# The recurrent part of a chunked mLSTM kernel turned around: v stationary, weights streaming, state term in PSUM, exponent bias on ScalarE

## The chip, the cores and the metric

The kernel runs on one core of one Trainium2 chip. The metric is the device time of one execution in microseconds (us). For each kernel one execution was also recorded by the hardware profiler; what is read from a trace is from that one execution, and what is said of times is from all runs.

## The reference

Two blocks follow one another. The first is a recurrent cell over 768 steps for 4 batches of 8 heads of 40 features:

```python
for t in range(S):                                   # S = 768, per batch and head, D = 40
    m_new  = maximum(f[t] + m, i[t])
    f_stab, i_stab = exp(f[t] + m - m_new), exp(i[t] - m_new);  m = m_new
    C = f_stab * C + i_stab * outer(v[t], k[t])      # 40 x 40 state
    n = f_stab * n + i_stab * k[t]
    y[t] = sigmoid(o[t]) * (C @ q[t]) / maximum(abs(n @ q[t]), 1.0)
# ... then, with x = y as (4, 768, 320):
u  = x + real(fft(fft(x, axis=1), axis=2))
un = (u - mean(u)) / sqrt(var(u) + 1e-6)
out = u + maximum(un @ w_ch1, 0) @ w_ch2             # 320 -> 1280 -> 320
```

## The kernel before

The cell is computed in 6 chunks of 128 steps per batch: inside a chunk as a masked product of scores and weights, between chunks through the state C. All heads of a batch go through one chunk together. The order of the program is batch 0 of the cell, the conversion of the feed-forward weights from float64, batch 1 of the cell, and then Fourier part and feed-forward part batch by batch, with the cell of batches 2 and 3 between them. A scheduler moves instructions, so that parts of neighbouring batches overlap.

This is the chunk, the part that the change touches (`hip` is 0 or 1 for the head of a pair: even heads lie in partitions 0 to 39, odd ones in 64 to 103):

```python
Mb = mbp.tile([L, H, L], FP, name="Mb", tag="Mb")          # running maximum, the same in every partition
nc.sync.dma_start(out=Mb, in_=M_d[c, heads, :].unsqueeze(0).to_broadcast([L, H, L]))
W = wp.tile([L, H, L], FP, name="W", tag="W")
nc.vector.tensor_tensor(out=W, in0=colT[:, c, 0, heads].unsqueeze(2).to_broadcast([L, H, L]), in1=Mb,
                        op=OP.subtract)
nc.gpsimd.affine_select(out=W, in_=W, compare_op=OP.is_ge, fill=MASKED, base=0, pattern=[[0, H], [1, L]],
                        channel_multiplier=-1)
nc.scalar.activation(out=W, in_=W, func=AF.Exp)
for hip in range(2):
    r = slice(hip * 64, hip * 64 + D)
    ps = ps_s.tile([L, NP, L], FP, name="ps", tag="ps")
    for p in range(NP):                                    # scores k x q
        nc.tensor.matmul(ps[:, p, :], qk[r, 1, p, :], qk[r, 0, p, :], start=True, stop=True)
    Wv = W.rearrange("p (pr two) t -> p pr two t", two=2)[:, :, hip, :]
    nc.vector.tensor_tensor(out=Wv, in0=ps, in1=Wv, op=OP.mult)
h1 = tp.tile([L, H, D1], FP, name="h1", tag="h1")
if c > 0:                                                  # the state's share
    pn = ps_h.tile([L, NP, 2 * D1], FP, name="pn", tag="ph")
    for p in range(NP):
        nc.tensor.matmul(pn[:, p, :], qk[:, 0, p, :], C[:, p].rearrange("p a b -> p (a b)"),
                         start=True, stop=True)
    # ... h1 = pn x g on VectorE
ph = ps_h.tile([L, H, D1], FP, name="ph", tag="ph")
for h in range(H):                                         # W loaded, v (41 columns) streams
    nc.tensor.matmul(ph[:, h, :], W[:, h, :], v1[:, h, :], start=True, stop=True)
# ... h1 = h1 + ph on VectorE
# ... vw = v x weight on GpSimd; pc = k x vw; C = C x decay + pc, both on VectorE
# ... den = 1 / max(|h1[:, :, 40]|, 1) on VectorE; so = so x den on GpSimd; x = h1 x so on VectorE
```

## Time and profile before

| | kernel before |
|---|---|
| median of 4 runs | 728.56 us (723.77 to 735.60) |
| profiled run, span | 733.6 us |
| TensorE, VectorE, ScalarE, GpSimd busy | 647.7, 288.7, 110.6, 125.5 us |
| half clock after the first clock record (162.1 us) | 95.7 us |

The traces record two values of TensorE's granted clock, 1.00 (full clock) and 0.50 (half clock). The runs of the kernel before differ by over 2%, and this follows the clock of TensorE. Among seven runs made beside e1 to e4, the fastest, 719.03 us, came with a mean granted clock of 0.959, and the slowest of those that count as fast, 727.73 us, with 0.945. A mean lower by 0.014 over some 723 us is about 20 us more at half clock, and the time grew by 8.7 us. So a microsecond at half clock costs this kernel about 0.43 us, an estimate.

The stages in the tables below are cut by events that both kernels have: "batch 0" ends with the last write of its x, "conversion" with the last conversion instruction on VectorE, "batch 1" with the first product pu of batch 0's Fourier part. "Batch 2 head" is from there to the first feed-forward product pm, "FF 0" the two feed-forward blocks, "batch 2 tail" from the end of their po to the next pu. Batch 3 and FF 1 are cut in the same way, and "rest" is all after it.

### The profile page before, as it was taken

To read this page: it belongs to the slowest core of one execution; us is meant where nothing else is said; L and a number is where in the kernel's file an instruction comes from. 1 tells how busy PE (TensorE), PEld (TensorE's weight loads), DVE (VectorE), ACT (ScalarE), POOL (GpSimd) and SP (SyncE) were. 2 spreads that over 40 slices of the span, in tenths; PEclk is the share of its full clock that TensorE was granted. 3 is DMA by queue.
4 is the path that set the end of the run, shared out by engine and by line. 5 is a ranking of instruction groups with operands and counts; after the bars stand their busy time and mean duration, and the time that the engine had idled before them with its cause. 6 is when DMAs were issued, how large, how long until landed. Compare 5 with 4: busy or idle time off the path is not lost.

```text
span 733.6 us, 6949 instructions
## 1 busy us (share of the span) xinstructions
PE 647.7 (88%) x2732; PEld 431.5 (59%) x2732; DVE 288.7 (39%) x570; ACT 110.6 (15%) x193; POOL 125.5 (17%) x109
## 2 busy tenths in 40 slices
PE   4978321389999999999999999999989999989998
PEld 3867311368677464687684464787645546645545
DVE  6454599997656101145543111154421011330110
ACT  4011143214131101001202101002010100011010
POOL 3121276662232000021302000020200000000000
PEclk9999999999895999986975999957999999999999
DMA  7354145625332000032211000010000000000000
GB/s 229 122 172 172 45 127 173 202 82 185 115 125 86 27 19 27 10 101 86 82 46 48 0 27 1 22 42 1 1 0 10 18 0 28 1 0 0 28 0 28
DMA packets 16113, 45.60 MB, mean 62 GB/s; under 512 B 1968, under 2 KB 5264, under 8 KB 15952
## 3 DMA queue, kind: packets, MB, share of 16 engines
q1 hardware_dynamic: 16080, 45.15, 19.0%
q8 instruction: 22, 0.36, 0.2%
q14 instruction: 11, 0.09, 0.0%
HBM read 41.11 MB, written 4.03 MB: 62 GB/s over the span
## 4 chain that ended last, share of the span: by engine, by line
PE 84%; DVE 10%; issue 4%; ACT 1%; DMA 0%; POOL 0%; DVEq 0%; ACTq 0%; POOLq 0%
PE pm L350 26%; PE po L362 18%; PE pu L322 9%; PE ph L219 8%; PE ps L205 8%; PE pz L300 6%; PE pn L213 4%; DVE m L164 2%; PE pzt L308 2%; PE put L342 2%; PE pc L232 2%; DVE m L168 1%; DVE e L163 1%; DVE e L169 1%; DVE e L160 1%
## 5 line engine op out<-in xcount | busy, mean ns | idle before, releaser
L350 PE MATMUL pm<-unT,w_sb 128*128 128x384 f32 (+1 forms) x480 | 194.2, 536 | 0.6 <-ACT unT L343 0.6
L350 PEld LDWEIGHTS pm<-unT,w_sb 128*128 128x128 f32 (+1 forms) x480 | 80.7, 194 | 111.1 <-issue 87.2
L362 PE MATMUL po<-w_sb,hT 128*128 128x320 f32 x480 | 131.3, 434 | 0.0
L219 PE MATMUL ph<-kvt,W 128*128 128x41 f32 x384 | 71.5, 352 | 50.0 <-DVE W L207 40.9
L362 PEld LDWEIGHTS po<-w_sb,hT 128*128 128x128 f32 x480 | 90.5, 190 | 41.1 <-issue 4.4
L219 PEld LDWEIGHTS ph<-kvt,W 128*128 128x128 f32 x384 | 68.1, 265 | 57.5 <-DVE W L207 43.0
L205 PE MATMUL ps<-qk 40*128 40x128 f32 x384 | 76.4, 383 | 15.1 <-DMA qk<-in_qkT 15.1
L354 DVE TENSOR_SCALAR hT<-pm 128x384 f32<-128x384 f32 x40 | 22.3, 558 | 165.1 <-PE pm L350 165.1
L205 PEld LDWEIGHTS ps<-qk 40*128 40x128 f32 x384 | 62.7, 267 | 20.6 <-issue 16.4
L365 DVE TENSOR_TENSOR ot<-po,u 128x320 f32<-128x320 f32 x24 | 11.8, 492 | 118.4 <-PE po L362 118.4
L322 PE MATMUL pu<-dd_sb,Z 128*128 128x320 f32 x192 | 56.3, 435 | 0.0
L227 POOL TENSOR_TENSOR vw<-kvt,colT 128x328 f32<-128x328 f32 x20 | 15.9, 794 | 207.3 <-issue 195.5
L199 ACT ACTIVATE W<-W 128x1024 f32<-128x1024 f32 x24 | 25.2, 1058 | 155.7 <-POOL W L197 155.7
L300 PE MATMUL pz<-ds_sb,eo 128*128 128x386 f32 (+1 forms) x96 | 45.8, 619 | 1.4 <-ACT Zt L277 1.0
L322 PEld LDWEIGHTS pu<-dd_sb,Z 128*128 128x128 f32 x192 | 36.1, 190 | 15.4 <-issue 0.8
L356 ACT ACTIVATE hT<-pm 128x384 f32<-128x384 f32 x40 | 19.6, 491 | 156.3 <-PE pm L350 156.3
L197 POOL TENSOR_SCALAR_AFFINE_SELECT W<-W 128x1024 f32<-128x1024 f32 x24 | 27.9, 1164 | 77.5 <-DVE W L195 30.7
L213 PEld LDWEIGHTS pn<-C,qk 128*128 128x128 f32 x160 | 31.8, 288 | 8.3 <-issue 7.6
L213 PE MATMUL pn<-C,qk 128*128 128x82 f32 x160 | 33.4, 378 | 2.1 <-DVE C L237 2.1
L207 DVE TENSOR_TENSOR W<-ps,W 128x512 f32<-128x512 f32 x48 | 32.0, 682 | 6.7 <-PE ps L205 3.7
L249 POOL TENSOR_TENSOR so<-so,den 128x320 f32<-128x320 f32 x24 | 20.0, 833 | 79.1 <-DVE den L247 79.1
L195 DVE TENSOR_TENSOR W<-colT,Mb 128x1024 f32<-128x1024 f32 x24 | 31.0, 1291 | 0.0
(84 smaller groups left out, 471.6 us busy)
## 6 DMA issues: line engine op xcount, KB each, us to landing
Mb<-M_d SPq DMA_DIRECT2D x24, 512.0 KB
kvt<-in_kv SPq DMA_DIRECT2D x24, 324.0 KB
qk<-in_qkT SPq DMA_DIRECT2D x48, 160.0 KB
raw<-in_w SPq DMA_DIRECT2D x9, 640.0 KB
so<-in_o SPq DMA_DIRECT2D x4, 960.0 KB
out<-ot SPq DMA_DIRECT2D x24, 160.0 KB
ds_sb<-in_dft_s SPq DMA_DIRECT2D x1, 1155.0 KB
dd_sb<-in_dft_d SPq DMA_DIRECT2D x1, 800.0 KB
```

The costliest lines, as they stand in the source:

```text
L195: nc.vector.tensor_tensor(out=W, in0=colT[:, c, 0, heads].unsqueeze(2).to_broadcast([L, H, L]), in1=Mb, op=OP.subtract)
L197: nc.gpsimd.affine_select(out=W, in_=W, compare_op=OP.is_ge, fill=MASKED, base=0, pattern=[[0, H], [1, L]], channel_multiplier=-1)
L199: nc.scalar.activation(out=W, in_=W, func=AF.Exp)
L205: nc.tensor.matmul(ps[:, p, :], qk[r, 1, p, :], qk[r, 0, p, :], start=True, stop=True)
L207: nc.vector.tensor_tensor(out=Wv, in0=ps, in1=Wv, op=OP.mult)
L213: nc.tensor.matmul(pn[:, p, :], qk[:, 0, p, :], C[:, p].rearrange("p a b -> p (a b)"), start=True, stop=True)
L219: nc.tensor.matmul(ph[:, h, :], W[:, h, :], v1[:, h, :], start=True, stop=True)
L300: nc.tensor.matmul(pz.rearrange("p a k -> p (a k)"), eo[:, par, j, ch * L:(ch + 1) * L], ds_sb[:, j, c0:c0 + 2 * n], start=(j == 0), stop= ...
L322: nc.tensor.matmul(pu, z, dd_sb[:, n, :], start=(n == 0), stop=(n == 4))
L350: nc.tensor.matmul(pu, w1_sb[r, ch, f * L:(f + 1) * L], unT[r, ch].rearrange("p c t -> p (c t)"), start=(ch == 0), stop=(ch == 2))
L354: nc.vector.tensor_scalar(out=ht, in0=pu, scalar1=0.0, scalar2=None, op0=OP.max)
L362: nc.tensor.matmul(po, hT[f][:, i * L:(i + 1) * L], w2_sb[:, f, :], start=(f == 0), stop=(f == NFF - 1))
```

## The change

The intent: W, with 128 columns, was loaded to stream only 41 columns of v. Now v, padded to 64 columns, is loaded and W streams, with the two heads of a pair in the two column halves of the array. The output comes out transposed, so the state's share can be added in the same PSUM buffer from queries scaled by g, and four transposes turn the result back. VectorE loses the subtraction, the product with g, the addition and the decay of C.

```diff
-        nc.vector.tensor_tensor(out=W, in0=colT[:, c, 0, heads].unsqueeze(2).to_broadcast([L, H, L]), in1=Mb,
-                                op=OP.subtract)
-        nc.gpsimd.affine_select(out=W, ..., fill=MASKED, ...)
-        nc.scalar.activation(out=W, in_=W, func=AF.Exp)
+        for h in range(H):
+            nc.scalar.activation(out=W[:, h, :], in_=Mb[:, h, :], func=AF.Exp, scale=-1.0,
+                                 bias=colT[:, c, 0, b * H + h:b * H + h + 1])
+        nc.gpsimd.affine_select(out=W, ..., fill=0.0, ...)
-        for hip in range(2):
-            for p in range(NP):
-                nc.tensor.matmul(ps[:, p, :], qk[r, 1, p, :], qk[r, 0, p, :], start=True, stop=True)
+        for p in range(NP):
+            for hip in range(2):
+                nc.tensor.matmul(ps[hip][:, p, :], qk[r, 1, p, :], qk[r, 0, p, :], start=True, stop=True)
-        if c > 0:
-            # pn = q x C on TensorE, h1 = pn x g on VectorE
-        for h in range(H):
-            nc.tensor.matmul(ph[:, h, :], W[:, h, :], v1[:, h, :], start=True, stop=True)
-        # h1 = h1 + ph on VectorE
+        if c > 0:
+            # Gb: two broadcast DMAs of g
+            nc.gpsimd.tensor_tensor(out=qg, in0=qk[:, 0], in1=Gb, op=OP.mult)
+            for p in range(NP):
+                nc.tensor.matmul(ph[:, p, :], C[:, p, :], qg[:, p, :], start=(p == 0), stop=False, ...)
+        for p in range(NP):
+            for hip in range(2):
+                nc.tensor.matmul(ph[hip * 64:hip * 64 + 64, p, :], v1[:, 2 * p + hip, :], W[:, 2 * p + hip, :],
+                                 start=(c == 0 and p == 0), stop=True, ...)
+        nc.scalar.copy(out=hT, in_=ph)
+        for p in range(NP):
+            nc.tensor.transpose(px[:, p, :], hT[:, p, :], ident)
-                    nc.vector.tensor_tensor(out=Cv, in0=Cv, in1=d, op=OP.mult)
+                    nc.gpsimd.tensor_tensor(out=Cv, in0=C[r, :, m], in1=d, op=OP.mult)   # into a second C buffer
 ... (buffers for Gb, qg and two C per batch; padding of v on the host; comments removed)
```

## The prediction

> **What bounds the kernel now.** I read the page's busy shares and chain, then groups by line, then the timeline of one chunk of the recurrent part, then the windows with their clock. TensorE is busy 88% and the chain lies on it for 84% of the span:
>
> ```profile
> PE 84%; DVE 10%; issue 4%; ACT 1%; DMA 0%; POOL 0%; DVEq 0%; ACTq 0%; POOLq 0%
> PE pm L350 26%; PE po L362 18%; PE pu L322 9%; PE ph L219 8%; PE ps L205 8%; PE pz L300 6%; PE pn L213 4%; DVE m L164 2%; PE pzt L308 2%; PE put L342 2%; PE pc L232 2%; DVE m L168 1%; DVE e L163 1%; DVE e L169 1%; DVE e L160 1%
> ```
>
> Most of it (pm, po, pu, pz) the change does not touch. The part it touches, ph + ps + pn + pc, is some 21% of 733.6 us, about 155 us for 24 chunks (4 batches of 6). Its groups:
>
> ```profile
> L219 PE MATMUL ph<-kvt,W 128*128 128x41 f32 x384 | 71.5, 352 | 50.0 <-DVE W L207 40.9
> L205 PE MATMUL ps<-qk 40*128 40x128 f32 x384 | 76.4, 383 | 15.1 <-DMA qk<-in_qkT 15.1
> L219 PEld LDWEIGHTS ph<-kvt,W 128*128 128x128 f32 x384 | 68.1, 265 | 57.5 <-DVE W L207 43.0
> ```
>
> 384 records for 192 products: each fp32 product is two loads and two matmuls. In ph the 128-column W is loaded to stream only 41 columns. One chunk of batch 0, in order of time on TensorE:
>
> ```profile
> 54.44 0.78 PE L232 MATMUL pc<-vw,kvt 128*40 128x41 f32 x16
> 55.87 3.21 PE L219 MATMUL ph<-kvt,W 128*128 128x41 f32 x14
> 59.01 2.67 PE L205 MATMUL ps<-qk 40*128 40x128 f32 x14
> 61.60 2.00 PE L213 MATMUL pn<-C,qk 128*128 128x82 f32 x8
> ```
>
> The next chunk's ph begins at 66.47: the period is 11.3 to 12.6 us, of which TensorE works about 9.3 and then waits 3 us while VectorE scales pn, decays C, makes x and multiplies W. The last view is the clock:
>
> ```profile
> 20.00:30.00 10.00, 10.00 (x59) 9.38 (x59) 5.41 (x12) 1.06 (x1) 2.51 (x3) 1.00 0.43 153
> ...
> 310.00:320.00 10.00, 10.00 (x73) 8.04 (x71) 3.12 (x7) 0.00 (x0) 0.73 (x1) 1.00 0.16 47
> ...
> 480.00:490.00 10.00, 10.00 (x54) 8.70 (x53) 4.28 (x9) 1.06 (x1) 1.78 (x2) 0.50 0.09 29
> ```
>
> The column after the five busy times is the granted clock. At 1.00 (310 to 320 us) ph goes at 0.112 us per record, at 0.50 (480 to 490) at 0.22. The 20 to 30 us window says 1.00 but runs 3.14 us per 14 records, the slow pace: no clock event is recorded before 162 us, so I take the first 160 us as half clock. After 162 us the clock falls to 0.50 for 95 us in seven pieces, nearly all within recurrent chunks, and one of them (377 to 401) also slows 13 us of pm.
>
> **What the Trainium skill says.** "TensorE: Matmul & The Clock Gate", Part 1, says the clock is gated between 4/8 and 8/8 by recent activity in windows of about 3.4 us; the trace agrees in its two values and in periods of low array use that precede each fall. "TensorEngine Tiling (Array Packing)", Performance Considerations, names exactly this change, the swap of stationary and streaming with column tiling when few columns stream, and its Key Properties say that tiles run in parallel but a change of mode drains. Before agrees: pc, whose heads alternate between partitions 0 and 64, starts its matmuls in pairs 6 ns apart (16 records in 0.44 us at full clock), and between groups of different form 0.13 to 0.2 us pass. "GPSIMD Engine Reference", Specifications, says GpSimd and VectorE contend for SBUF interfaces. Before agrees: in the weight conversion a tensor_scalar of 0.49 us takes 1.75 to 1.83 us while a GpSimd tensor_tensor runs.
>
> **The change part by part**, per chunk; full clock first, half clock in brackets.
>
> TensorE. ph had 16 records x 0.112 = 1.8 us (3.6). Now v with 64 columns is loaded, W's 128 columns stream, and the two heads of a pair sit in different column halves. By ps, 128 streamed columns cost 0.107 us per record (0.213); in pairs 8 x 0.107 = 0.86 (1.7). ps: 16 x 0.107 = 1.7 (3.0 measured, partly paired); the change alternates the row halves, which would halve it, but the order of the built program still puts two or three products of one half in a row, so I count 1.2 (2.2). pn: 1.05 (1.95) becomes the state term, 8 x 0.11 = 0.9 (1.75). New: four transposes; put's go at 0.213 us each at half clock, so 0.43 (0.85). pc unchanged, 0.45 (0.7). With some six changes of form at 0.15: 4.7 us (8.0) against 5.4 (9.3).
>
> VectorE loses W = bias - M (1.29), pn x g (0.50), h + ph (0.50) and the decay of C (2 x 0.46): 3.2 of 6.5 us. ScalarE gains eight exponents of 128 columns for one of 1024 (1.06): its copies of 128 and 256 columns take 0.26 and 0.37, so 8 x 0.26 = 2.1, and a 512-column copy, 0.6. GpSimd gains qg (128x512, about 1.2) and the decay (0.9): 4.9 us instead of 2.8. DMA gains Gb, 256 KB, and 92 KB of padded v, where it is mostly 0.1 to 0.4 busy: hidden.
>
> The new recurrent loop is a chain of handovers. At half clock: W ready, ph 1.7 + 0.3 to drain; ScalarE copy 0.7; transposes 1.25; pc behind them and den, C + pc, reciprocal on VectorE, 1.75; so x den on GpSimd 0.9; x 0.75; two W products 1.3. Sum 8.65. The order also puts ps of the next chunk between the first ph product and the other seven, which are ready late, so about 9.5. At full clock: ph 1.2, copy 0.7, transposes 0.8, pc to reciprocal 1.6, so 0.9, x 0.8, W 1.3: 7.3, say 7.5.
>
> By stage (times of before):
> - 20 to 82 us, batch 0: about four loops at 11.6 become 9.5, chunk 0 gains 0.5: **-9**.
> - 82 to 152, weight conversion, VectorE 99% busy: about 5 us less VectorE work, but GpSimd's 2 to 4 us more block VectorE in turn: **-2**.
> - 152 to 196, batch 1 beside pz: 43.5 us for four loops; now 4 x 8.3 with pz in most gaps, + 3: **-7**.
> - 213 to 234 and 316 to 355, batch 2: 60 us. The new order moves chunks 1 to 5 behind the last po with little pz among them: 8 + 4 x 8.8 + 12 for pz and pzt after = 55: **-5**.
> - 371 to 388 and 475 to 516, batch 3, 57 us and 6.5 us lost by pm at half clock: 9 + 4 x 8.2 + 7 = 49, and part of the pm loss: **-10**.
> - The rest, 516 to 734 and the four pm/po blocks: nothing.
>
> Sum -33: 730.6 - 33 = **697 us**.
>
> **The rivals.** (1) *Clock stays up.* Per chunk, streamed columns weighted by rows used rise from some 5,200 to 9,800 cycles in no more time. The falls followed 3.4 us stretches where this was below about 0.43 of a full array; in the stages with pz it should now stay above. If the clock held everywhere, loops of 7.5 and no slow pm: another 15 to 20 us, some 678. Against: copy, den and x leave over 3 us in which TensorE has little to do, so a stage without pz may fall to half just before its ph. (2) *Latency takes the place of the work.* Every output passes TensorE, ScalarE, TensorE, VectorE, GpSimd, VectorE before the next W product. If handovers cost 0.25 us more each, loops of 10.5 to 11 leave only batches 0 and 3 better: 715 to 720. Speaking for it: batch 2 becomes five chunks in a row without filler. (3) *GpSimd becomes the bound.* 4.9 us of a 9 us loop is not full, but it is in order and qg, mask and decay stand ahead of so x den; with VectorE contention, 5 to 15 us worse. (4) *Buffer wait.* ph, px and pc share two PSUM buffers. The built program lets the state term wait only for the new C, not for x, so I give this little. (5) *Pairs don't overlap* in ph because they write one bank: ph 1.7 (3.4), +10 to 15 us. pc speaks against it.
>
> **Range and chances.** Prediction 697; the clock rival sets the low end, 672, latency and GpSimd together the high end, 720. Faster by over 2% means below 716: 0.77. Same 0.19, slower 0.04.
>
> **What would show it.** ph matmuls should start in pairs a few ns apart and take about 0.9 us per chunk at full clock. In batch 0 ph should recur every 9 to 10 us; TensorE should wait for W (VectorE), the transposes for h (ScalarE). The granted clock should be 0.50 for well under 95 us after 162 us. The conversion should be no more than 5 us shorter. GpSimd's busy time should be near 165 us (125 before). The prediction is wrong if the loop exceeds 10.5 us, if pm again starts at half clock for long, if GpSimd's queue, not the transposes, holds x, or if ph's heads run one after the other.

## More of the kernel before

The page cuts the span into 40 slices of 18.3 us. Here are TensorE's busy share and its granted clock, in tenths (9 is 90% or more):

```profile
PE   4978321389999999999999999999989999989998
PEclk9999999999895999986975999957999999999999
```

The clock row is to be read with care. The first clock record of this trace is at 162.1 us, in the ninth slice; before it the row shows 9 because nothing is recorded. The falls to 5 to 8 behind it lie where the cell of batches 1 to 3 runs.

## The result

The changed kernel takes **693.15 us** (median of 4 runs, 691.57 to 694.67) against 728.56 us before. The ratio is 0.9537, with a 95% interval of 0.9492 to 0.9582. A ratio here is the mean time of one kernel's runs over the mean of the other's runs of the same rounds, so it is not quite the ratio of the two medians. Executions over 1.5% slower than the fastest of the same kernel are left out of the means. The total lies 4 us from the predicted 697. The way there does not.

The page of the changed kernel, the chain and the groups that answer to those of before:

```profile
PE 77%; DVE 9%; issue 7%; POOL 5%; ACT 1%; DMA 0%; POOLq 0%; DVEq 0%; ACTq 0%
PE pm L362 27%; PE po L374 19%; PE pu L334 9%; PE ps L210 5%; PE ph L229 4%; PE pz L312 4%; PE ph L225 2%; DVE m L167 2%; PE px L235 2%; PE pzt L320 2%; PE put L354 2%; POOL qg L223 1%; PE pc L245 1%; DVE e L166 1%; DVE e L165 1%
...
L229 PE MATMUL ph<-W,kvt 128*64 128x128 f32 x384 | 40.3, 329 | 38.0 <-DVE W L213 30.9
L210 PE MATMUL ps<-qk 40*128 40x128 f32 x384 | 62.3, 360 | 27.8 <-DMA qk<-in_qkT 14.9
L229 PEld LDWEIGHTS ph<-W,kvt 128*64 128x64 f32 x384 | 29.3, 164 | 46.0 <-DVE W L213 33.4
L225 PE MATMUL ph<-qg,C 128*128 128x128 f32 x160 | 28.2, 330 | 11.9 <-POOL qg L223 11.0
```

The busy time of ph fell from 71.5 to 40.3 us. GpSimd has come into the chain with 5%, and the state's share (L225) waits 11 us in all for the scaled queries. The windows at the same three times as in the prediction:

```profile
20.00:30.00 10.00, 7.50 (x53) 5.78 (x54) 2.54 (x8) 3.54 (x11) 4.88 (x6) 1.00 0.90 215
310.00:320.00 10.00, 9.49 (x115) 7.87 (x116) 5.22 (x15) 3.58 (x11) 7.15 (x10) 1.00 0.65 203
480.00:490.00 10.00, 10.00 (x38) 6.74 (x36) 3.98 (x11) 0.00 (x0) 0.00 (x0) 1.00 0.00 0
```

From 310 to 320 us TensorE now runs 115 matmuls in place of 73. The third window falls into another stage than before, but its clock of 1.00 stands for the whole trace: of 95.7 us of half clock after the first record, 13.7 us are left. Batch 0 looks different. Here is one of its chunks, TensorE alone, in order of time:

```profile
53.91 2.08 PE L225 MATMUL ph<-qg,C 128*128 128x128 f32 x8 [2.79 <-POOL qg L223]
55.91 0.69 PE L229 MATMUL ph<-W,kvt 128*64 128x128 f32 x2
56.53 1.22 PE L210 MATMUL ps<-qk 40*128 40x128 f32 x4
57.68 1.97 PE L229 MATMUL ph<-W,kvt 128*64 128x128 f32 x14
59.58 1.65 PE L210 MATMUL ps<-qk 40*128 40x128 f32 x8
61.16 1.11 PE L235 MATMUL px<-ident,h 128*128 128x128 f32 x4
62.20 0.78 PE L245 MATMUL pc<-vw,kvt 128*40 128x41 f32 x16
62.90 0.80 PE L210 MATMUL ps<-qk 40*128 40x128 f32 x4
66.49 2.08 PE L225 MATMUL ph<-qg,C 128*128 128x128 f32 x8 [2.78 <-POOL qg L223]
```

The loop is 12.58 us (53.91 to 66.49): TensorE works 9.8 us without a gap and then waits 2.8 us. In the kernel before, the last three loops of batch 0 were 11.3 to 12.6 us. **Batch 0 gained nothing**, although ph itself is shorter.

The stages of the profiled runs, in us, with the experiments that the argument rests on (all of one execution each). The scheduler does not leave every chunk in the same stage: two chunks of batch 2 and two of batch 3 stand in the heads of the kernel before, one of each in those of the changed kernel, and the rest in the tails. So heads and tails are best read together.

| stage | before | after | e1 | e4 | f4 | g2 | g3 | g4 |
|---|---|---|---|---|---|---|---|---|
| batch 0 | 84.1 | 86.7 | 85.1 | 69.3 | 85.4 | 78.2 | 67.6 | 66.2 |
| conversion | 67.5 | 64.8 | 67.6 | 64.9 | 68.3 | 63.6 | 64.1 | 63.9 |
| batch 1 | 43.4 | 40.3 | 49.4 | 40.2 | 46.3 | 41.0 | 54.6 | 39.5 |
| batch 2 head | 38.8 | 24.6 | 25.8 | 24.7 | 25.2 | 27.6 | 25.8 | 26.8 |
| FF 0 | 82.3 | 80.5 | 81.2 | 80.4 | 80.9 | 80.5 | 81.2 | 80.8 |
| batch 2 tail | 39.3 | 37.0 | 40.9 | 37.0 | 42.4 | 39.5 | 40.9 | 38.5 |
| batch 3 head | 33.0 | 28.2 | 29.3 | 25.4 | 27.0 | 23.9 | 29.4 | 24.6 |
| FF 1 | 86.8 | 80.6 | 80.8 | 80.6 | 80.7 | 80.5 | 80.7 | 80.8 |
| batch 3 tail | 40.4 | 30.9 | 34.9 | 30.9 | 33.8 | 38.5 | 34.9 | 35.4 |
| rest | 218.0 | 219.4 | 219.4 | 219.3 | 219.2 | 217.8 | 219.2 | 217.1 |
| span | 733.6 | 693.0 | 714.4 | 672.7 | 709.2 | 691.1 | 698.4 | 673.6 |

Of the 40.6 us between the two profiled runs, 38.8 lie in batches 2 and 3 with their feed-forward blocks, and 3.2 in batch 0, the conversion and batch 1 together; the rest lost 1.4.

Half clock by stage, from the same traces, says more than the totals. The time up to the first record is counted as half clock, since the products of the recurrent part run at the slow pace there (ph 0.215 us apart before). It fills batch 0 and the conversion of both kernels. In batch 1 it takes 17.3 us of the kernel before and 4.2 us of the changed one, in batches 2 and 3 with their feed-forward blocks 85.3 and 6.8 us.

### The profile page after: what moved, and what is told of

Its sections match the earlier page's. It is cut to its first block, busy times and chain, and to the rows that moved or that the text cites. A ratio compares the mean times of both kernels' runs of the same rounds, so it can differ in the third digit from the quotient of the medians.

```text
span 693.0 us, 7416 instructions
## 1 busy us (share of the span) xinstructions
PE 597.1 (86%) x2822; PEld 375.7 (54%) x2822; DVE 222.2 (32%) x470; ACT 157.6 (23%) x386; POOL 159.2 (23%) x163
## 4 chain that ended last, share of the span: by engine, by line
PE 77%; DVE 9%; issue 7%; POOL 5%; ACT 1%; DMA 0%; POOLq 0%; DVEq 0%; ACTq 0%
PE pm L362 27%; PE po L374 19%; PE pu L334 9%; PE ps L210 5%; PE ph L229 4%; PE pz L312 4%; PE ph L225 2%; DVE m L167 2%; PE px L235 2%; PE pzt L320 2%; PE put L354 2%; POOL qg L223 1%; PE pc L245 1%; DVE e L166 1%; DVE e L165 1%
## 5 line engine op out<-in xcount | busy, mean ns | idle before, releaser
L374 PEld LDWEIGHTS po<-w_sb,hT 128*128 128x128 f32 x480 | 90.8, 190 | 40.9 <-issue 4.4
L210 PE MATMUL ps<-qk 40*128 40x128 f32 x384 | 62.3, 360 | 27.8 <-DMA qk<-in_qkT 14.9
L229 PE MATMUL ph<-W,kvt 128*64 128x128 f32 x384 | 40.3, 329 | 38.0 <-DVE W L213 30.9
L210 PEld LDWEIGHTS ps<-qk 40*128 40x128 f32 x384 | 47.6, 236 | 39.3 <-issue 34.1
L200 ACT ACTIVATE W<-Mb,colT 128x128 f32<-128x128 f32 x192 | 59.2, 391 | 3.9 <-DVE den L258 2.3
L229 PEld LDWEIGHTS ph<-W,kvt 128*64 128x64 f32 x384 | 29.3, 164 | 46.0 <-DVE W L213 33.4
L232 ACT COPY h<-ph 128x512 f32<-128x512 f32 x24 | 14.0, 584 | 127.5 <-PE ph L229 127.5
L225 PE MATMUL ph<-qg,C 128*128 128x128 f32 x160 | 28.2, 330 | 11.9 <-POOL qg L223 11.0
L312 PE MATMUL pz<-ds_sb,eo 128*128 128x386 f32 (+1 forms) x96 | 35.7, 503 | 0.3 <-issue 0.3
L223 POOL TENSOR_TENSOR qg<-qk,Gb 128x512 f32<-128x512 f32 x20 | 26.0, 1301 | 39.6 <-PE ph L225 38.1
L225 PEld LDWEIGHTS ph<-qg,C 128*128 128x128 f32 x160 | 24.6, 232 | 17.4 <-POOL qg L223 14.2
```

The source lines that it names most:

```text
L200: nc.scalar.activation(out=W[:, h, :], in_=Mb[:, h, :], func=AF.Exp, scale=-1.0, bias=colT[:, c, 0, b * H + h:b * H + h + 1])
L210: nc.tensor.matmul(ps[hip][:, p, :], qk[r, 1, p, :], qk[r, 0, p, :], start=True, stop=True)
L223: nc.gpsimd.tensor_tensor(out=qg, in0=qk[:, 0], in1=Gb, op=OP.mult)
L225: nc.tensor.matmul(ph[:, p, :], C[:, p, :], qg[:, p, :], start=(p == 0), stop=False, skip_group_check=True)
L229: nc.tensor.matmul(ph[hip * 64:hip * 64 + 64, p, :], v1[:, 2 * p + hip, :], W[:, 2 * p + hip, :], start=(c == 0 and p == 0), stop=True, sk ...
L312: nc.tensor.matmul(pz.rearrange("p a k -> p (a k)"), eo[:, par, j, ch * L:(ch + 1) * L], ds_sb[:, j, c0:c0 + 2 * n], start=(j == 0), stop= ...
```

## The experiments

All outputs are right. The changed kernel was not run again beside them: what is compared is each one's ratio to the kernel before in its own rounds, with 0.9537 for the changed kernel. The kernel before had medians of 726.74 us beside e1 to e4, 733.59 beside f1 to f4 and 733.62 beside g1 to g4. Two ideas stood at the start. Theory A: in batches 2 and 3 the gain is mostly the clock, and batch 0 is slow because GpSimd's queue holds the loop. Rival: the layout itself gives the gain, and batch 0 is held by handovers.

### e1: the kernel before, kept at full clock in batches 1 to 3

```diff
+            if b >= 1:
+                for _ in range(2):   # hot_w, hot_x: constant bf16 tiles; the result is overwritten by the scores
+                    nc.tensor.matmul(ps.rearrange("p a t -> p (a t)"), hot_w, hot_x, start=True, stop=True)
```

> The kernel before with four dummy bf16 matmuls of 512 columns per chunk of batches 1 to 3 (overwritten at once, results unchanged). Theory A (the clock carries most of the gain of batches 2 and 3): the dummies cost about 0.85 us per chunk at full clock, 18 chunks, 15 us of TensorE, but the granted clock stays 1.00 after 162 us, so 95 us at half clock vanish, worth 25 to 45 us: the time falls by 10 to 30 us, to 700 to 720. Theory B (it is the smaller TensorE work of the new form): the clock may stay up, but the time is the same as before or 5 to 15 us longer.

Measured: 715.90 us (713.54 to 716.17), ratio 0.9876 (0.9813 to 0.9939). More work made the old kernel faster. The clock row of its page:

```profile
PEclk9999999999899999999999999999999999999999
```

Half clock after the first record fell from 95.7 to 13.8 us. In the table, batch 2 head fell from 38.8 to 25.8 us (one of its two chunks moved into the tail, which grew by only 1.6 us) and FF 1 from 86.8 to 80.8, nearly the values of the changed kernel; batch 3 head and tail lost 9.2 us together. Over batches 2 and 3 and their feed-forward blocks this run takes 292.9 us, the kernel before 320.6 and the changed kernel 281.8. So 27.7 of those 38.8 us are to be had with the old layout. That the clock gives them, and not the new order of chunks, is checked by its price: 85.3 us of half clock at 0.43 are 36.7 us, less some 10 us of idle products (12 chunks x 4 x 0.21) 26.7 us, an estimate. Batch 1 paid 6 us, and the idle products brought no clock there: it was at half clock for 20.8 us, against 17.3 before.

### e2: the gate product on VectorE

```diff
-        nc.gpsimd.tensor_tensor(out=sc, in0=sc, in1=den.unsqueeze(2).to_broadcast([L, H, D]), op=OP.mult)
+        nc.vector.tensor_tensor(out=sc, in0=sc, in1=den.unsqueeze(2).to_broadcast([L, H, D]), op=OP.mult)
```

GpSimd in the changed kernel, in the chunk shown above (decay, gate product, next scaled queries, next mask):

```profile
63.42 0.99 POOL L253 TENSOR_TENSOR C<-C,decB 40x164 f32<-40x164 f32 x2 [7.82 <-DVE C L254]
64.49 0.72 POOL L261 TENSOR_TENSOR so<-so,den 128x320 f32<-128x320 f32 x1
65.17 1.26 POOL L223 TENSOR_TENSOR qg<-qk,Gb 128x512 f32<-128x512 f32 x1
66.39 1.09 POOL L202 TENSOR_SCALAR_AFFINE_SELECT W<-W 128x1024 f32<-128x1024 f32 x1
```

GpSimd stood idle for 7.82 us and then did all four in a row; the state's share could start only behind qg, at 66.49. That looked like the cause.

> The changed kernel with the product of the output gate and 1/den on VectorE instead of GpSimd, so that qg and the mask no longer stand behind it in GpSimd's queue. Theory A (batch 0 and 1 are held by GpSimd's in-order queue: so, then qg, then mask, then the W product): the period of ph in batch 0 falls from 12.6 to about 9.5 to 10 us and that of batch 1 from 9 to about 8, some 10 to 14 us in all, to about 680. Theory B (half clock and the handovers hold it): 12.6 us falls by under 1 us and the time by under 5 us.

Measured: 690.43 us (690.14 to 693.72), ratio 0.9542 (0.9478 to 0.9605), the same as the changed kernel. The middle loops of batch 0 were 11.1, 12.0 and 12.0 us, each about 0.5 us shorter than the 11.6, 12.6 and 12.6 of the changed kernel, and batch 0 took 82.2 us instead of 86.7 in the trace; little of it is left in the total. Theory B holds, and GpSimd's queue is a small part. The decay still stood before the scaled queries here. No run moved both products away at half clock, so what the queue costs there in all stays open: TensorE's waits for the scaled queries in batch 0 of the changed kernel are 7.9 us in all.

### e3: the scaled queries on VectorE

```diff
-            nc.gpsimd.tensor_tensor(out=qg, in0=qk[:, 0], in1=Gb, op=OP.mult)
+            nc.vector.tensor_tensor(out=qg, in0=qk[:, 0], in1=Gb, op=OP.mult)
```

> The changed kernel with the scaled queries made on VectorE instead of GpSimd. Theory A (GpSimd's queue): 1.3 us per loop leaves it, batch 0 period 12.6 to about 11.3 us, some 5 to 8 us in all, but the VectorE-bound conversion may get up to 2 us longer. Theory B: no change within 3 us.

Measured: 700.92 us (695.87 to 701.49), ratio 0.9653 (0.9569 to 0.9737), about 8 us worse than the changed kernel, which neither theory said. Batch 0 took 86.1 us in the trace; the loss was in batch 1 (42.2 us), batch 2 tail (38.9) and batch 3 tail (34.5). Why was not followed further. With e2 it says that the queue of GpSimd, though it is in the chain, is not what a single move can relieve.

### e4: the changed kernel, kept at full clock in batch 0

```diff
+        if b == 0 and c > 0:
+            for hip in range(2):
+                for _ in range(4):
+                    nc.tensor.matmul(ps[hip].rearrange("p a t -> p (a t)"), hot_w, hot_x, start=True, stop=True)
```

> The changed kernel with eight dummy bf16 matmuls of 512 columns per chunk 1 to 5 of batch 0, overwritten at once. Theory A (GpSimd's queue holds batch 0, the half clock adds to it): if the clock goes up, ph, px and copies get about 1.5 to 2 us shorter per loop and the dummies mostly fill idle time: 5 to 10 us less in all; if it does not go up, up to 10 us more. Theory B (clock alone makes batch 0 slow): period falls from 12.6 to below 9.5, 15 us less.

Measured: 679.17 us (674.37 to 683.87), ratio 0.9376 (0.9295 to 0.9456). The first clock record is now at 26 us, and the row shows full speed in batch 0 and half clock only behind it, in the conversion:

```profile
PE   4697103189999999999999999999999999899998
PEclk9998555589999999999999999999899999999999
```

Batch 0 fell from 86.7 to 69.3 us, with 1.8 us of idle work added per chunk (8 products of 0.22 us). The transposes are 0.109 us apart where they were 0.231. So batch 0 of the changed kernel had been at half clock, and this was what it was short of. The conversion, at half clock as well, kept its 65 us: it does not wait for TensorE.

### f1: gate product and decay on VectorE, with e4's idle products

```diff
 # e4, and
+        nc.vector.tensor_tensor(out=sc, in0=sc, ...)                      # was gpsimd
+                    nc.vector.tensor_tensor(out=Cv, in0=C[r, :, m], ...)  # was gpsimd
```

> The changed kernel with the eight idle bf16 products per chunk in batch 0 (as in the run that took 679.2 us) and with the two GpSimd products that wait for the current chunk moved to VectorE: output gate times reciprocal, and state times decay. Correct result. Theory A (in-order GpSimd queue): in the changed kernel the next chunk's scaled queries (1.27 us) and mask (1.09 us) stand behind the decay (2 x 0.46 us) and the gate product (0.72 us), which wait for this chunk's state and denominator; with those gone GpSimd runs ahead, the batch-1 loop falls from 9.3-9.6 us to about 6.5, and the time to 655-668 us. Theory B (the loop is bound by its own latency or by the DMA queue): batch-1 loop stays above 8.5 us and the time within 674-684 us. Theory C (VectorE takes the queue's place): slower than 684.

Measured: 676.33 us (673.52 to 680.21), ratio 0.9246 (0.9179 to 0.9312). Theory A falls: the loops of batch 1 were 8.3 to 9.7 us and the time is B's. The shares of the chain between 145 and 164 us, two loops of batch 1, tell why:

```profile
by line: PE pz L320 29.3%; PE ps L218 19.1%; PE ph L237 17.8%; PE pzt L328 11.8%; PE ph L233 9.4%; PE px L243 6.5%; PE pc L253 4.6%; DVE W L221 3.2%; issue 0.4%
```

With GpSimd out of the way TensorE is full, and 41% of it is the Fourier part of batch 0 (pz and pzt), which the scheduler puts there. Batch 1 took 37.6 us instead of 40.2; batch 3 head and tail gave back 7.7, with 13.7 us of half clock there and in FF 1, where e4 had none. The queue of GpSimd is worth 2.6 us in batch 1, no more.

### f2: the kernel before with idle products everywhere, first try

```diff
 # e1, and in batch 0
+            if b >= 1 or c > 0:
+                for _ in range(2 if b >= 1 else 4):      # four in front of each half of the scores
```

> The kernel before with idle bf16 products in all four batches (eight per chunk from the second on in batch 0, four per chunk in batches 1 to 3), so that TensorE is at full clock in every recurrent stage. Correct result. Beside the changed kernel with its batch 0 kept at full clock (679.2 us) this shows what the layout alone is worth. Theory A (the half clock in batch 0 costs both layouts alike): batch 0 shrinks by 10-17 us against the run with idle products in batches 1 to 3 only (715.9 us), so 698-706 us, and the layout is worth 20-27 us at full clock. Theory B (batch 0 of the kernel before is bound by VectorE and latency, not by TensorE's clock): 711-720 us, and the layout is worth 32-41 us at full clock.

Measured: 737.21 us (724.84 to 738.18); three of four runs, the profiled one too, count as slow. The windows view of 30 to 60 us, in batch 0 (busy times of TensorE, its loads, VectorE, ScalarE, GpSimd, then the clock as recorded):

```profile
30.00:60.00 30.00, 30.00 (x138) 22.53 (x136) 11.21 (x26) 2.11 (x2) 5.09 (x6) 1.00 0.32 102
```

TensorE was busy all the time and the clock did not rise: the idle products came 0.42 us apart, twice the 0.22 of e4, and those of ph 0.215. The run decides nothing about the old layout at full clock.

Busy time hides what differs here. Count instead the columns that stream, each weighted by the share of the 128 rows that it uses and doubled for fp32, and divide by what fits into 3.41 us, the length of the shortest clock records, at full clock (po streams 320 fp32 columns, so 640, in 0.269 us). Then such stretches of this run from 31 to 58 us hold 0.22 to 0.37 of a full array, those of g3 below 0.54 to 0.66, and those of e4 from 26 to 43 us 0.78 to 0.88, an estimate.

### f3: the scores in the old order

```diff
-        for p in range(NP):
-            for hip in range(2):
+        for hip in range(2):
+            for p in range(NP):
```

> The changed kernel with the score products issued in the old order, all four pairs of one half of the rows and then all of the other, instead of alternating halves. Correct result. Theory A (alternating halves lets two 40-row products run at once and this is on the path): the 8-record stretch of score products goes from 0.53 us to 0.9 or more, and the time rises by 6 to 17 us, to 699-710 us. Theory B (score products are made ahead and wait for nobody): their records lengthen but the time stays within 690-697 us. Theory C: the lower use of the array in a window also brings the half clock back in batches 2 and 3: over 710 us.

Measured: 689.15 us (688.83 to 690.89), ratio 0.9422 (0.9364 to 0.9480). Alternating the row halves brings nothing; the old order is even a little faster. In its trace batch 0 took 82.6 us instead of 86.7, with three pieces of full clock (6.8, 3.4 and 3.4 us from 34 us on) where the changed kernel had none. Eight score records took 0.93 us against 0.72 to 0.94 in the changed kernel at the same place, so even the records hardly changed, and nobody waited for them.

### f4: the old exponents in the changed kernel

```diff
-        for h in range(H):
-            nc.scalar.activation(out=W[:, h, :], in_=Mb[:, h, :], func=AF.Exp, scale=-1.0, bias=colT[...])
+        nc.vector.tensor_tensor(out=W, in0=colT[:, c, 0, heads]..., in1=Mb, op=OP.subtract)
         # mask with MASKED in place of 0.0
+        nc.scalar.activation(out=W, in_=W, func=AF.Exp)
```

> The changed kernel with the exponent path of the kernel before: one subtraction on VectorE for all heads (1.29 us), mask with -10000 on GpSimd, one exponential of 1024 columns on ScalarE (1.06 us), instead of eight exponentials with a bias and a mask of zeros. Correct result. Theory A (the exponents are made a chunk ahead; the change only moves 31 us from VectorE to 34 us more of ScalarE, both off the path): within 690-697 us, but batch 0, where VectorE is 50 to 60 per cent busy, may give back 1 to 3. Theory B (VectorE's in-order queue is in the loop): 700-712 us.

Measured: 712.28 us (711.07 to 721.38), ratio 0.9761 (0.9680 to 0.9841). Theory B holds: the exponents on ScalarE are worth some 16 us of the profiled span, which is as much as the whole rest of the change (0.9761 against 1). The loss lies in the conversion (3.5 us), batch 1 (6.0), batch 2 tail (5.4) and batch 3 tail (2.9). The group of the subtraction shows what it waits for:

```profile
L200 DVE TENSOR_TENSOR W<-colT,Mb 128x1024 f32<-128x1024 f32 x24 | 32.2, 1341 | 10.8 <-PE ph L229 8.7 <-DMA Mb<-M_d 2.0
```

It can start only when ph has let go of a W buffer, and then VectorE, GpSimd and ScalarE follow one after the other before the score product. In the changed kernel the same stretch is ScalarE and GpSimd. That this shorter stretch is the reason is argued from the trace; that the part is worth 16 us is measured. A rival stands beside it: in f4 batch 1 was at half clock for 24.4 us and batch 2 tail for 6.8, in the changed kernel for 4.2 and 0, and these two stages make up 11.4 us of the loss. How much comes straight from the longer stretch and how much by way of the clock, no run separates; the 3.5 us of the conversion, at half clock in both, is not the clock.

### g1: the new exponents in the kernel before

```diff
 # the reverse of f4, in the kernel before
```

> The kernel before with the exponent part of the change alone: eight exponentials of 128 columns with the bias on ScalarE and a mask of zeros, in place of the subtraction on VectorE, the mask of -10000 and one exponential of 1024 columns. Correct result. With the run before this one, in which the changed kernel was given the old exponents back and lost some 16 to 19 us, it completes a table of two by two. Theory A (the subtraction on VectorE is in the recurrent loop of either layout, so the parts add up): 12-19 us faster than the kernel before, a ratio of 0.974-0.984, most of it in the conversion and in batch 1. Theory B (in the old layout VectorE's other work hides it or the half clock of TensorE decides): ratio 0.990-1.005.

Measured: 735.33 us (730.48 to 739.58), ratio 1.0058 (0.9981 to 1.0136). Theory B: the same part that is worth 16 us in the new layout is worth nothing in the old one. In the trace the old layout still lost 88.8 us to half clock after its first record, and its batch 1 took 47.6 us, 25.6 of them at half clock (43.4 and 17.3 in the kernel before). The parts of this change do not add up, as long as the clock is left free to differ.

### g2: the products v x W one column half after the other

```diff
-        for p in range(NP):
-            for hip in range(2):
+        for hip in range(2):
+            for p in range(NP):
                 nc.tensor.matmul(ph[hip * 64:hip * 64 + 64, p, :], ...)
```

> The changed kernel with the products v x W issued one column half after the other (four heads of the left half of the array, then four of the right) instead of alternating. Correct result. Theory A (only alternating heads overlap, and ph lies on the path): the 16 records of ph go from 1.02 us to about 1.7 us at full clock (1.8 to 3.4 at half), and the time rises by 10 to 22 us, ratio to before 0.968-0.985. Theory B (pairs overlap in any order, or ph is hidden): ratio 0.948-0.960, as the changed kernel (0.954).

Measured: 692.98 us (692.80 to 694.05), ratio 0.9464 (0.9411 to 0.9516): as fast as the changed kernel. But theory B's reason is wrong, and A's is half right. Here is ph of one chunk of batch 2 at full clock, in the changed kernel and then in this one:

```profile
299.37 1.09 PE L229 MATMUL ph<-W,kvt 128*64 128x128 f32 x16
```

```profile
302.93 1.09 PE L229 MATMUL ph<-W,kvt 128*64 128x128 f32 x8
304.77 1.09 PE L229 MATMUL ph<-W,kvt 128*64 128x128 f32 x8 [0.75 <-DVE W L213]
```

Alternating heads do overlap: 16 records in the time that 8 take otherwise. Batches 2 and 3 with their feed-forward blocks took 290.5 us against 281.8, so the overlap is worth some 8.7 us there, in single traces; the variants that leave it alone lie between 279.0 (e4) and 288.9 (f1), so the figure is rough. Batch 0 gave it back: 78.2 us against 86.7. The clock records show how. They begin at 34 us, and four stretches of 3.4 us at full speed (34.4, 44.6, 54.8 and 65.1 us) lie in four successive loops of 10.2 us. In the changed kernel no loop of batch 0 reached full clock. That the slower order kept the array busier, and that the clock rose for it, is argued: counted as in f2, the stretches before these four held 0.53 or 0.54 of a full array, but others at up to 0.54 in batch 0 of the changed kernel brought no full clock.

### g3: the kernel before with idle products everywhere, second try

```diff
 # e1, and in batch 0, from the second chunk on, ten in front of the first half of the scores
+            n = 2 if b >= 1 else 10 * (1 - hip) * (c > 0)
```

> The kernel before with idle bf16 products again, this time ten per chunk of batch 0 in front of one half of the score products (the run with four and four left batch 0 at half clock: each idle product took 0.42 us, not 0.21), and four per chunk in batches 1 to 3. Correct result. To be read by the pace inside batch 0, not by the total. Theory A (batch 0 of the old layout is bound by TensorE at half clock): if idle products take 0.21 us there, ph's records go from 0.215 to about 0.11 us apart, the loop from 11.6-12.6 to 9-10.5 us even with the idle work, total 705-715 us. Theory B (bound by VectorE and handovers): the loop stays at 11.5 or more although the clock is full. If the idle products again take 0.42 us the run decides nothing, at 735-745 us.

Measured: **698.03 us** (695.35 to 701.47), ratio 0.9524 (0.9449 to 0.9598). This time the clock rose, and the time is below the 705 to 715 us that theory A expected. The same window as in f2, twice the matmuls:

```profile
30.00:60.00 30.00, 29.92 (x274) 22.85 (x272) 23.13 (x53) 4.92 (x5) 8.72 (x10) 1.00 0.60 224
```

One of its loops in batch 0, on TensorE:

```profile
45.79 1.47 PE L211 MATMUL ps<-hot_x,hot_w 128*128 128x512 bf16 x6
47.10 1.76 PE L227 MATMUL ph<-kvt,W 128*128 128x41 f32 x14
48.78 0.51 PE L240 MATMUL pc<-vw,kvt 128*40 128x41 f32 x16
49.22 1.04 PE L211 MATMUL ps<-hot_x,hot_w 128*128 128x512 bf16 x4
50.19 1.71 PE L213 MATMUL ps<-qk 40*128 40x128 f32 x16
51.83 1.12 PE L221 MATMUL pn<-C,qk 128*128 128x82 f32 x8
```

The loop is 7.2 us, with 2.2 us of it idle products, and no wait is left: VectorE's long queue does not show. Batch 0 takes 67.6 us, as in the changed kernel at full clock (69.3 in e4). Theory A holds: the old layout in batch 0 was bound by TensorE at half clock, and at full clock the two layouts are alike there. The whole kernel with the old layout comes to the time of the changed one. It would be lower still without the loss of 11.2 us in batch 1, where the idle products did not keep the clock up (32.4 of 54.6 us at half clock): an estimate, 698.4 minus 11.2, is 687 us. Against the 672.7 us of e4 this leaves some 14 us for the change itself, exponents and layout together, when batches 0, 2 and 3 run at full clock in both, an estimate from single traces.

### g4: a version meant to beat both

```diff
 # the changed kernel with five and five idle products per chunk from the second on in batch 0, and
+        (nc.vector if b < 2 else nc.gpsimd).tensor_tensor(out=sc, ...)
+                    (nc.vector if b < 2 else nc.gpsimd).tensor_tensor(out=Cv, in0=C[r, :, m], in1=d, op=OP.mult)
```

> A version meant to beat both: the changed kernel with ten idle bf16 products per chunk from the second on in batch 0, and the gate product and the decay on VectorE in batches 0 and 1 only (in all batches they took 2.6 us off batch 1 and cost 5 to 8 us in batches 2 and 3). Correct result. Theory: batch 0 ends at 68-70 us, batch 1 takes 37-38 us, batches 2 and 3 as in the changed kernel, so 668-675 us, ratio to before 0.915-0.930. If the split brings nothing: 676-682 us.

Measured: **674.85 us** (672.92 to 677.11), ratio 0.9214 (0.9159 to 0.9269). It beats both kernels. Batch 0 (66.2 us) is better than expected; batch 1 (39.5) and batch 3 tail (35.4) are not, so that it stays within the noise of f1 and e4. Nearly all of the gain over the changed kernel lies in batch 0 (66.2 us against 86.7), and e4 shows that to be mostly the clock.

## Why the prediction was right or wrong

The total was right, 697 against 693.15 us, by luck: batch 0, the conversion and batch 1 gained 15 us less than forecast, batches 2 and 3 with FF 1 22 us more. Its sum also starts from 730.6 us, which is one of the four runs (730.63); the median is 728.56. By its own steps:

| step | predicted, us | measured, us |
|---|---|---|
| batch 0 | -9 | +2.6 |
| conversion | -2 | -2.7 |
| batch 1 | -7 | -3.1 |
| batch 2 head and tail | -5 | -16.5 |
| batch 3 with FF 1 | -10 | -20.5 |
| FF 0 and rest | 0 | -0.4 |

- **"A stage without pz may fall to half": batch 0.** The step that failed is the sum of TensorE's work at half clock, "4.7 us (8.0)". At full clock it was good: in g4 the parts of a chunk are 1.16 (state) + 1.52 (ph) + 1.16 (ps) + 0.60 (transposes) + 0.51 (pc) = 4.95 us, and in g3 those of the old layout 2.15 + 1.71 + 1.12 + 0.51 = 5.5 against "5.4". At half clock the scores took 3.7 us, not 2.2, ph 2.7, not 1.7, the state term 2.1, not 1.75, and the transposes 1.1, not 0.85; the run of work without a gap is 9.8 us, as long as before. The loop followed, 12.6 us in place of 9.5.
- **"Chain of handovers".** At half clock TensorE's own row of work is in series with most of it, and the only wait that shows is the one for the scaled queries, 2.8 us. "If the loop exceeds 10.5" the prediction called itself wrong, and for this stage it was. e4 shows what was missing: 17.4 us lay in the clock.
- **Conversion.** Right in size and reason: with VectorE's subtraction put back (f4) it was 3.5 us longer.
- **Batch 1.** The prediction took it for the layout. Without the new exponents (f4) the stage takes 6.0 us longer, 2.9 us more than before. But the clock moves with it: half clock took 17.3 of 43.4 us before, 4.2 of 40.3 in the changed kernel and 24.4 of 46.3 in f4, so exponents, layout and clock are not separated here. The loops stayed at 9.2 to 10.5 us, because TensorE carries pz and pzt of batch 0 (f1) and waits for GpSimd.
- **Batches 2 and 3: rival (1), "clock stays up".** It was named, its mark was right ("well under 95 us", measured 13.7), and it was left out of the prediction's number. e1 puts it at 27.7 us of the 38.8 there, after paying for its own idle products. The rival's measure holds up too: counted as in f2, the seven falls of the kernel before follow stretches at 0.32 to 0.43 of a full array, and in batches 2 and 3 the changed kernel goes as low only once while at full clock. It is no rule: four other stretches of the kernel before at 0.39 to 0.43 brought no fall, nor did that one (0.41), and the one fall of the changed kernel there followed a stretch at 0.56. "Loops of 7.5" were 4.9 to 6.7 us in the trace, as masks, scaled queries and weights there are made ahead.
- **Rival (2), latency**: not seen as the bound; at full clock batch 0 falls to 7 to 8 us per loop in either layout (g4 and g3, all loops but the first). **Rival (3), GpSimd's queue**: it is in the chain, but in another order than described: decay and gate product stand ahead of qg and the mask, and what waits is the state term, 2.8 us per loop, rather than x. e2 and f1 price it at 0 to 3 us of the total; e3 only moved the work to VectorE and lost. **Rival (4), buffer wait**: not seen, the state term waits for qg (11.0 of its 11.9 us of idle time). **Rival (5), no overlap in pairs**: false; g2 shows the overlap, worth some 8.7 us in batches 2 and 3, and the same kernel gains 8.5 us in batch 0, where the clock rose.
- **Eight exponents.** They were priced at 8 x 0.26 = 2.1 us. They take 2.44 us, a start every 0.29 us and 390 ns for one; the Trainium skill, "ScalarE: Activation LUTs", section "What ACT_TABLE_LOAD costs", gives about 280 ns + 0.833 ns per column for an activation with a bias per partition, which is 387 ns for 128 columns. The trace agrees, and the page would have given the right figure. That this part is worth 16 us was nowhere in the prediction, which counted it only as load on VectorE.

What stays open: why e3 was slower, how f4's 16 us divide between the longer stretch and the clock, why batch 1 of the old layout stays at half clock so long, and how much of the gain in batches 2 and 3 beyond the clock (281.8 us against e1's 292.9) is e1's own idle work. That is at most 12 chunks x 4 x 0.21 = 10 us, an estimate from e1's count of products and their pace, so the clock may be nearly the whole gain there.

## What to carry to other kernels

Before counting instructions, find out at which clock each stage runs, from the pace of a known product and not from the clock row alone, because here most of a change's gain was a matter of the clock, and the stage where it failed was held by the clock in both layouts. When a stage runs at half clock, a few idle products are a cheap experiment (e1, e4, g3): they tell whether the stage lacks work or lacks clock, and may be worth more than the rewriting. Test a change's parts in both settings, since a part worth 16 us in one layout was worth nothing in the other, and look at the clock of each setting before calling it the part's own worth.

## What the Trainium skill lacked or had wrong

- "TensorE: Matmul & The Clock Gate", section "Why this matters for your kernels", advises no idle gaps of over about 3 us between bursts. The advice is not enough here: in f2 TensorE had no gap from 30 to 60 us and stayed at half clock (idle products 0.42 us apart), and in the changed kernel the wait was 2.8 us per loop and the clock stayed at half for all of batch 0. The page does not say how narrow or short products count as activity; g2 (four stretches of 3.4 us at full clock, changed kernel none) shows that it matters.
- The same page, Part 1, puts the penalty of the warm-up ramp at under 1% of a typical kernel span. That is said of the first microseconds of steady work, and as a budget it would mislead here: the slow pace lasted until 162.1 us in the kernel before, and in batch 0 alone it cost 16.5 us of 733.6, over 2% (84.1 us against 67.6 in g3, which carries idle products besides).
- No page says that the profile's clock shows full speed before its first record. Here the first record is at 155.7 us in the changed kernel and 162.1 us in the kernel before, while in batch 0 the transposes of the changed kernel are 0.231 us apart (0.109 at full clock in e4) and the records of ph in the kernel before 0.215 (0.113 in g3): half clock throughout.
- "TensorEngine Tiling (Array Packing)", section "Theoretical Speedup", gives up to 2x for two column tiles. For ph at full clock this is what the runs show (16 records in the 1.09 us of 8), but a gain of the array is not one of the kernel: serial order gave the same time, 692.98 against 693.15 us.
